# Hashed attention and a convolved feed-forward block on one core: inverse sums by full transposes, key and query loads by head, and a weight's GpSimd part one unit later

## The chip, the cores and the metric

The kernel runs on one NeuronCore of a Trainium2 chip. The metric is the device time of one execution in microseconds (us): the median over three runs is 740.17 us, the runs lying between 739.85 and 744.33.

## What is computed

Attention over 4 batches, 8 heads, 768 positions and head width 64, where a query sees only the keys that fall in its hash bucket (six sign bits of a projection), then a feed-forward block with a three-tap convolution along the sequence. Everything is float32, cut here to what matters:

```python
q_bucket = sum((q @ proj > 0) * 2**arange(6));  k_bucket likewise
scores = where(q_bucket[..., :, None] == k_bucket[..., None, :], q @ k.T / 8, -1e9)
e = exp(scores - max(scores));  x = (e / (sum(e) + 1e-9)) @ v      # (B, S, 512) after joining heads
h = relu(x @ w_in)                                                 # 512 -> 1024
gate = sigmoid(conv_w[0]*h[s-1] + conv_w[1]*h[s] + conv_w[2]*h[s+1])
out = (h * gate) @ w_out                                           # 1024 -> 512
```

The weights arrive as float64 and are decoded on the chip into a high and a low float32 part.

## The kernel before

**Pairs, units and bursts.** Two heads make a pair; there are 16 pairs. A pair has 12 units, k = 0 to 11. A unit is 128 queries of one head against all 768 keys. The main loop (L453) issues, for unit i: the score products of unit i on TensorE (`products`, L257), the row maximum on VectorE, which also moves the scores from PSUM to SBUF (`maximum`, L270), the transposes of unit i-3 on TensorE (L297) with their copy by ScalarE (L304), and the exponential of unit i on ScalarE (L277). Every fourth unit (k = 3, 7 and 11) is a burst: TensorE also multiplies the transposed weights of 256 queries with the values (`values`, L307, 24 matmul records at L325).

**Inverse sums.** For the first seven pairs the division by the sum of exponentials is done after the product with the values. VectorE reduces the partial sums to four numbers per partition and takes their reciprocals (`reciprocals`, L291 and L292, a tile of 128x4), two units ahead of the burst. At the head of the burst, `spread` (L319) lets TensorE bring each of the four columns, broadcast to 64 columns, into the layout of the output: four matmuls of 64 output partitions, two records each. ScalarE copies the result out (L330), VectorE multiplies (`out`, L333), GpSimd splits into a high and a low part (`parts`, L336 and L337). The other nine pairs ("late") divide ahead of the transposes, on GpSimd (`normalise`, L285), and have no spread.

**Preparing the next pair.** The raw queries and keys of the next pair lie in one tile `R` (128 x 2 heads x 768), which has a single buffer. For each head GpSimd makes the high part (L171) and then the low part in place (L176), and SP's DMA queue moves the pieces to where the products read them (L174, L178). The four steps are issued at k = 1, 3, 5 and 7. TensorE computes the hash of both heads at k = 3 (L186), with VectorE's sign test behind it (L189). At k = 7, behind the last low part, SP gets the values' load of the next pair (L165) and then the load of `R` for the pair after it (L158).

**Weights.** The 16 weight blocks are decoded in the background of the first seven pairs. Each block takes six VectorE instructions (L91 to L101), then a cast on ScalarE (L110), then two GpSimd instructions (L111, L112). `background` is called in the bursts, 5.2 steps each (4.2 at k = 3). In a burst GpSimd's queue therefore gets the two weight instructions first, then the `parts` of the output, then the low part of `R`.

**PSUM.** Scores and transposes share three slots in turn, so that the transposes of one unit take the slot of the unit before, and cannot start until VectorE's maximum of that unit has read it.

The feed-forward block of a batch (`ffn`, L412) runs between two units, first when pair 6 is done (221 us into the span).

Of the kernel before, what the change touches and what calls it, by code (L numbers as in the profile page):

```python
# [17 lines left out]
P = 128  # L18
# [3 lines left out]
QB = 256  # L22
# [12 lines left out]
PREP = 1  # L35
PREP_N = 6
W0 = 7
# [5 lines left out]
def lsh_attention_conv_ffn(ctx, tc, qk, v, hw, w_in, conv_w, w_out, consts, ident_in, out):  # L43
# [8 lines left out]
    def ring(pool, bufs, shape, dtype, tag, name):  # L52

        k = turns[tag] = (turns.get(tag, -1) + 1) % bufs
        return pool.tile(shape, dtype, tag=f"{tag}{k}", name=name, bufs=1)
# [47 lines left out]
    def split_weights():  # L103

        while fetched:
            raw, name = fetched.pop(0)
            d = Decode(raw, WC, name)
            yield from d.vector()
            blk = weights[name] = cp.tile([P, 2, WC], F32R, tag=f"w{name}", name=f"w{name}")
            nc.scalar.copy(blk[:, 0, :], d.upf)  # L110
            nc.gpsimd.tensor_tensor(d.upf, d.upf, blk[:, 0, :].bitcast(F32), ALU.subtract)  # L111
            nc.gpsimd.tensor_tensor(blk[:, 1, :], d.upf, d.lowf, ALU.add)  # L112
            yield

# [9 lines left out]
    blocks += [(w_out[f * P:(f + 1) * P], f"o{f}") for f in range(NFC)]  # L124
    fetched, taps, due = [], [], [0]
    weights_todo = split_weights()
# [17 lines left out]
    class Pair:  # L144
        def __init__(self, b, p):
            self.b, self.p, self.nm = b, p, f"{b}_{p}"
            self.late = b * NP + p >= LATE
            self.inv = None

        def load(self):  # L150
            nm = self.nm
            self.R = ring(wp, 1, [P, 2, S], F32R, "R", f"R{nm}")
            src = qk[self.b, 2 * self.p:2 * self.p + 2].rearrange("h p s -> p h s")
            if self.b == self.p == 0:
                for h in range(2):
                    nc.sync.dma_start(self.R[:, h].bitcast(F32), src[:, h])
            else:
                nc.sync.dma_start(self.R.bitcast(F32), src)  # L158
            self.Q1 = ring(wp, 2, [P, 2, S], F32R, "Q1", f"Q1{nm}")
            self.K1 = ring(wp, 2, [P, 2, S], F32R, "K1", f"K1{nm}")  # L160
            self.Q2, self.K2 = Q2s[self.p % 2], K2s[self.p % 2]
# [5 lines left out]
        def split(self, h):  # L167

            lo, R = self.R[:, h], self.R[:, h].bitcast(F32)
            hi = ring(wp, 1, [P, S], F32R, "hi", f"hi{self.nm}_{h}")  # L170
# [9 lines left out]
        def hash(self):  # L180
            hp = ring(ps, 3, [P, 2, 512], F32, "S", f"hash{self.nm}")
            R = self.R.bitcast(F32)
            for h in range(2):
                for half in range(2):
                    g = 32 * (2 * h + half)
                    nc.tensor.matmul(hp[g:g + 32, 0, :HS], hw_sb[:, :32], R[:, h, half * HS:(half + 1) * HS],  # L186
                                     start=True, stop=True, tile_position=(0, g))
# [22 lines left out]
        def prepare_now(self):  # L210
# [3 lines left out]
            for h in range(2):  # L214
                hps.append(ring(ps, 2, [P, 512], F32, "M", f"hash{nm}_{h}")[:, :HS])
                for g in range(4):
                    c, half = 32 * (1 + g // 2), g % 2
                    nc.tensor.matmul(hps[h][32 * g:32 * g + 32], hw_sb[:, c:c + 32],
                                     self.R[:, h, half * HS:(half + 1) * HS].bitcast(F32),
                                     start=True, stop=True, tile_position=(0, 32 * g))  # L220
            for h in range(2):
                R = self.R[:, h].bitcast(F32)
                Q1, Q2, K1, K2 = (t[:, h] for t in (self.Q1, self.Q2, self.K1, self.K2))
# [21 lines left out]
    class Unit:  # L245
# [41 lines left out]
        def reciprocals(self):  # L287

            pr = self.pair
            pr.inv = ring(wp, 2, [P, 2 * QB // P], F32, "inv", f"inv{self.nm}")  # L290
            nc.vector.tensor_reduce(pr.inv, self.sums, mybir.AxisListType.X, ALU.add)  # L291
            nc.vector.reciprocal(pr.inv, pr.inv)  # L292

# [13 lines left out]
    def values(pr, qb, ats, inv):  # L307
# [7 lines left out]
        def spread():  # L315

            for t in range(QB // P):
                for h in range(2):
                    nc.tensor.matmul(av[h * D:(h + 1) * D, QB + t * P:QB + (t + 1) * P],  # L319
                                     inv[:, 2 * t + h:2 * t + h + 1].to_broadcast([P, D]), ident,  # L320
                                     start=True, stop=True, tile_position=(0, h * D))

# [89 lines left out]
    def ffn(b, xs, fill, last):  # L412
# [4 lines left out]
        for i in range(len(todo) + FLAG):  # L417
# [5 lines left out]
            if i == 0:  # L423
                fill()
            background(1)
            if i >= 3:
                prepare(0)
                prepare(1)
# [6 lines left out]
            if i < len(todo):  # L435
# [5 lines left out]
             for t in range(qb * QB // P, (qb + 1) * QB // P)]  # L441
    pairs[0].load()
    nc.sync.dma_start(ident, ident_in)
# [4 lines left out]
    next(first)  # L448
    pairs[1].load()
    av, outs, lows, early = [], [], [], None  # L450
    n = len(units)
    ffn_after = {min((b + 1) * NP - 1 + DEFER, B * NP - 1): b for b in range(B)}
    for i in range(n + LAG):  # L453
# [55 lines left out]
        prepare(1)  # L509
        if u and k == PREP + PREP_N and pi + 1 < len(pairs):  # L510
            pairs[pi + 1].load_v()
            if pi + 2 < len(pairs):
                pairs[pi + 2].load()
        if i == 3:
# [66 lines left out]
```

## Time and profile before

| | |
|---|---|
| runs | 739.85, 740.17, 744.33 us |
| the profiled execution's own time | 739.48 us |
| its span, first to last instruction | 737.5 us |
| TensorE matmul records | 710.9 us busy, 96% of the span |
| VectorE | 487.3 us, 66% |
| ScalarE | 498.5 us, 68% |
| GpSimd | 331.9 us, 45% |
| mean granted TensorE clock | 0.997 |

Engines: PE is TensorE's matmuls, PEld its weight loads, DVE is VectorE, ACT ScalarE, POOL GpSimd, SPq the DMA queue of the sync engine. A share of busy time is a mean over stages; what an engine holds up is read from the waits and from the timeline of a stretch. A row of the timeline gives the start, the time to the end of its last instruction, the engine, the line, the operation, output and inputs, the number of instructions, and in brackets the idle time ahead with what ended it. TensorE's matmuls overlap, so that the distance from one row's start to the next one's start is what a piece of its work costs.

### The profile page before, as it was taken

Reading aid. Unit: us, or ns where it says so; the run is one execution under the profiler, and the core shown is the slowest. Engines: PE = TensorE matmul, PEld = TensorE weight load, DVE = VectorE, ACT = ScalarE, POOL = GpSimd, SP = SyncE. Lnnn points to the kernel's source line nnn. Section 1 sums busy time; section 2 is a strip of 40 time slices with the busy share of each in tenths; the row PEclk is TensorE's granted clock in tenths of the full one; section 3 lists DMA queues with packets and bytes.
Section 4 is the critical chain, followed back from the end, with each engine's and each line's share of the span. In section 5 each row is a group of like instructions: output and inputs, shape, how many; then the busy total and the mean of one; then the engine's idle time right before and its main releaser. Section 6 shows DMA issues by size and latency. Waiting matters only on the chain.

```text
span 737.5 us, 13543 instructions
## 1 busy us (share of the span) xinstructions
PE 710.9 (96%) x4720; PEld 589.0 (80%) x4720; DVE 487.3 (66%) x1211; ACT 498.5 (68%) x937; POOL 331.9 (45%) x334
## 2 busy tenths in 40 slices
PE   6998999899899999999999999999999999999997
PEld 3787777678778988777877998778778899878996
DVE  7977878788775755666665666466666566555663
ACT  5788578678684554877877554778778655585554
POOL 4265456357463522475673532355755232241321
PEclk9999999999999999999999999999999999999999
DMA  4867666663552310237545130324463001100011
GB/s 143 222 187 202 165 186 166 165 166 89 147 146 52 86 44 36 72 77 189 139 105 149 34 94 3 108 60 113 117 180 95 1 0 44 44 1 1 0 44 43
DMA packets 30355, 72.17 MB, mean 98 GB/s; under 512 B 5936, under 2 KB 7504, under 8 KB 30288
## 3 DMA queue, kind: packets, MB, share of 16 engines
q1 hardware_dynamic: 27696, 62.88, 32.0%
q10 hardware_dynamic: 2592, 8.44, 3.3%
q8 instruction: 37, 0.61, 0.3%
q14 instruction: 30, 0.25, 0.1%
HBM read 27.40 MB, written 6.29 MB: 46 GB/s over the span
## 4 chain that ended last, share of the span: by engine, by line
PE 69%; DMA 11%; POOL 7%; issue 5%; DVE 4%; SPq 3%; ACT 1%; POOLq 0%; DVEq 0%; ACTq 0%
PE h L368 19%; PE o L398 18%; PE v L325 11%; PE s L257 10%; PE t L297 9%; DMA R<-in_qk 6%; DMA k<-R 4%; POOL R L176 2%; SPq L174 2%; DVE e L270 1%; DMA K<-hi 1%; PE hash L186 1%; POOL hi L171 1%; ACT e L277 1%; SPq L178 1%
## 5 line engine op out<-in xcount | busy, mean ns | idle before, releaser
L270 DVE TENSOR_SCALAR_CACHE_REDUCE e<-s 128x768 f32<-128x768 f32 x192 | 183.2, 954 | 81.2 <-PE s L257 70.6
L277 ACT ACTIVATE e<-e,st 128x768 f32<-128x768 f32 x192 | 181.3, 944 | 10.3 <-DVE st L284 5.0
L304 ACT COPY at<-t 128x768 f32<-128x768 f32 x192 | 152.3, 794 | 47.0 <-PE t L297 47.0
L297 PE MATMUL t<-ident,e 128*128 128x128 f32 x1152 | 160.0, 275 | 3.6 <-POOL e L285 1.5
L377 DVE SCALAR_TENSOR_TENSOR ht<-ht,cw 128x384 f32<-128x384 f32 (+1 forms) x128 | 114.7, 896 | 71.2 <-ACT ht L375 69.0
L387 POOL TENSOR_TENSOR g<-ht,g 128x384 fp32r<-128x384 f32 x64 | 71.5, 1117 | 179.5 <-ACT g L386 141.8
L297 PEld LDWEIGHTS t<-ident,e 128*128 128x128 f32 x1152 | 130.6, 141 | 22.3 <-POOL e L285 7.4
L285 POOL TENSOR_SCALAR e<-e,st 128x768 f32<-128x768 f32 x108 | 98.3, 911 | 103.1 <-DVE st L284 51.4
L398 PE MATMUL o<-wo,g 128*128 128x512 f32 x576 | 142.4, 394 | 0.0
L368 PE MATMUL h<-xh,wi 128*128 128x386 f32 x512 | 141.9, 340 | 0.0
L325 PE MATMUL v<-at,v 128*64 128x256 f32 x1152 | 135.6, 385 | 0.0
L398 PEld LDWEIGHTS o<-wo,g 128*128 128x128 f32 x576 | 107.4, 188 | 20.3
L257 PE MATMUL s<-K,Q 128*128 128x384 f32 x384 | 116.7, 385 | 1.9 <-ACT e L277 1.0
L325 PEld LDWEIGHTS v<-at,v 128*64 128x64 f32 x1152 | 81.2, 138 | 42.4 <-issue 8.6
L257 PE MATMUL s<-k,q 96*128 96x384 f32 x384 | 100.2, 342 | 2.1 <-ACT q L237 1.9
L368 PEld LDWEIGHTS h<-xh,wi 128*128 128x128 f32 x512 | 94.1, 188 | 4.8 <-issue 1.8
L380 ACT ACTIVATE ht<-ht 128x384 f32<-128x384 f32 x64 | 33.6, 526 | 91.4 <-DVE ht L377 91.4
L368 PE MATMUL h<-xl,wi 128*128 128x386 f32 x256 | 86.7, 339 | 0.0
L257 PEld LDWEIGHTS s<-K,Q 128*128 128x128 f32 x384 | 59.0, 192 | 23.2 <-issue 16.6
L257 PEld LDWEIGHTS s<-k,q 96*128 96x128 f32 x384 | 70.7, 191 | 3.5 <-ACT q L237 3.0
L381 DVE TENSOR_TENSOR ht<-ht 128x384 f32<-128x384 f32 x64 | 40.2, 629 | 33.4 <-ACT ht L380 33.4
L176 POOL TENSOR_TENSOR R<-R,hi 128x768 fp32r<-128x768 f32 x30 | 56.6, 1886 | 0.2
(75 smaller groups left out, 586.0 us busy)
## 6 DMA issues: line engine op xcount, KB each, us to landing
R<-in_qk SPq DMA_DIRECT2D x15, 768.0 KB
K<-hi SPq DMA_DIRECT2D x60, 192.0 KB
v<-in_v SPq DMA_DIRECT2D x16, 384.0 KB
out<-osb SPq DMA_DIRECT2D x24, 256.0 KB
Q<-hi SPq DMA_DIRECT2D x30, 192.0 KB
q<-hi SPq DMA_DIRECT2D x30, 192.0 KB
Q<-R SPq DMA_DIRECT2D x30, 192.0 KB
k<-R SPq DMA_DIRECT2D x30, 192.0 KB
```

The lines of the kernel that those rows point to most:

```text
L176: nc.gpsimd.tensor_tensor(lo, R, hi.bitcast(F32), ALU.subtract)
L257: nc.tensor.matmul(self.sp[:, half, :HS], A[:, h, qs], C[:, h, half * HS:(half + 1) * HS], start=(kk == 0), stop=(kk == 1))
L270: nc.vector.tensor_scalar(self.e.rearrange("p (a b) -> p a b", a=2), self.sp[:, :, :HS], MASKED, None, ALU.max, ALU.max, accum_out=self.st ...
L277: nc.scalar.activation(self.e, self.e, AF.Exp, bias=self.st[:, 1:2], scale=SCALE, accum_out=self.sum)
L285: nc.gpsimd.tensor_scalar(self.e, self.e, self.st[:, 3:4], 0.0, ALU.mult, ALU.add)
L297: nc.tensor.transpose(self.tp[:, c // 3, c % 3 * P:(c % 3 + 1) * P], self.e[:, c * P:(c + 1) * P], ident)
L304: nc.scalar.copy(pr.at[self.h][:, :, :, self.tq * P:(self.tq + 1) * P], self.tp[:, :, :3 * P].rearrange("p j (c q) -> p j c q", c=3))
L325: nc.tensor.matmul(av[h * D:(h + 1) * D, :QB], vt[:, c, h, :], ats[h][:, c // 3, c % 3, :], start=(c == 0), stop=(c == NCK - 1), tile_posi ...
L368: nc.tensor.matmul(hp[:, :HW], w, x[:, c0:c0 + HW], start=(n == 0), stop=(n == 3 * NCC - 1))
L377: nc.vector.scalar_tensor_tensor(t[:, a:z], ht[:, o + k - 1 + a:o + k - 1 + z], cw[:, f, k:k + 1], t[:, a:z], ALU.mult, ALU.add)
L387: nc.gpsimd.tensor_tensor(g[:, 1, :], t, g[:, 0, :].bitcast(F32), ALU.subtract)
L398: nc.tensor.matmul(op, l, r, start=(f == 0 and n == 0), stop=(f == NFC - 1 and n == 2))
```

## The change

There are three parts.

1. `reciprocals` now writes the four reciprocals spread out: the sums go to a tile `total` of 128x4, and one VectorE reciprocal reads it with each number broadcast 64 times and writes a tile `inv` of 128x256. `spread` is two transposes of 128x128 instead of four matmuls of 64 output partitions.
2. `R` is two tiles, one per head. Their loads are issued at k = 7 and k = 8, and the values' load moves behind the second. The hash reads the two tiles in turn.
3. A weight block's two GpSimd instructions are taken out of the burst: the cast puts the block on a list `cast`, and `low_weights` issues them at the end of the next unit that isn't a burst (in the feed-forward block at once).

```diff
-PREP_N = 6
+PREP_N = 6,7
...
             nc.scalar.copy(blk[:, 0, :], d.upf)
+            cast.append((d, blk))
+            yield
+
+    def low_weights():
+
+        for d, blk in cast:
             nc.gpsimd.tensor_tensor(d.upf, d.upf, blk[:, 0, :].bitcast(F32), ALU.subtract)
             nc.gpsimd.tensor_tensor(blk[:, 1, :], d.upf, d.lowf, ALU.add)
-            yield
+        cast.clear()
...
-        def load(self):
+        def load(self, h):
+
             nm = self.nm
-            self.R = ring(wp, 1, [P, 2, S], F32R, "R", f"R{nm}")
-            src = qk[self.b, 2 * self.p:2 * self.p + 2].rearrange("h p s -> p h s")
-            if self.b == self.p == 0:
-                for h in range(2):
-                    nc.sync.dma_start(self.R[:, h].bitcast(F32), src[:, h])
-            else:
-                nc.sync.dma_start(self.R.bitcast(F32), src)
+            self.R[h] = ring(wp, 1, [P, S], F32R, f"R{h}", f"R{nm}_{h}")
+            nc.sync.dma_start(self.R[h].bitcast(F32), qk[self.b, 2 * self.p + h])
+            if h == 0:
+                return
...
         def reciprocals(self):
 
             pr = self.pair
-            pr.inv = ring(wp, 2, [P, 2 * QB // P], F32, "inv", f"inv{self.nm}")
-            nc.vector.tensor_reduce(pr.inv, self.sums, mybir.AxisListType.X, ALU.add)
-            nc.vector.reciprocal(pr.inv, pr.inv)
+            total = ring(wp, 2, [P, 2 * QB // P], F32, "total", f"total{self.nm}")
+            nc.vector.tensor_reduce(total, self.sums, mybir.AxisListType.X, ALU.add)
+
+            pr.inv = ring(wp, 1, [P, QB], F32, "inv", f"inv{self.nm}")
+            nc.vector.reciprocal(pr.inv.rearrange("p (a d) -> p a d", d=D),
+                                 total.unsqueeze(2).to_broadcast([P, 2 * QB // P, D]))
...
             for t in range(QB // P):
-                for h in range(2):
-                    nc.tensor.matmul(av[h * D:(h + 1) * D, QB + t * P:QB + (t + 1) * P],
-                                     inv[:, 2 * t + h:2 * t + h + 1].to_broadcast([P, D]), ident,
-                                     start=True, stop=True, tile_position=(0, h * D))
+                nc.tensor.transpose(av[:, QB + t * P:QB + (t + 1) * P], inv[:, t * P:(t + 1) * P], ident)
...
         prepare(1)
-        if u and k == PREP + PREP_N and pi + 1 < len(pairs):
+        if not burst:
+            low_weights()
+        if u and k - PREP in PREP_N and pi + 2 < len(pairs):
+            pairs[pi + 2].load(PREP_N.index(k - PREP))
+        if u and k - PREP == PREP_N[1] and pi + 1 < len(pairs):
             pairs[pi + 1].load_v()
-            if pi + 2 < len(pairs):
-                pairs[pi + 2].load()
```

How the instructions stand on three queues follows. A name carries the number of its pair within the batch, or of its weight block, and ends in a serial number.

GpSimd's queue from a burst at k = 3 to the burst at k = 7, where the next pair, the first of batch 1, is being prepared. Before:

```order
L111 TENSOR_TENSOR upi_1_1199<-upi_1_1199,wi_1_1320 128x512
L112 TENSOR_TENSOR wi_1_1320<-upi_1_1199,lowi_1_1198 128x512
L336 TENSOR_SCALAR xh_2_1030<-rs_2_1_1154 128x256
L337 TENSOR_TENSOR xl_2_1031<-rs_2_1_1154,xh_2_1030 128x256
L176 TENSOR_TENSOR R_0_1089<-R_0_1089,hi_0_0_1247 128x768
L191 TENSOR_SCALAR bits_0_1299<-bits_0_1299,cst 128x384
L171 TENSOR_SCALAR hi_0_1_1383<-R_0_1089 128x768
L111 TENSOR_TENSOR upi_1_1325<-upi_1_1325,wi_1_1453 128x512
L112 TENSOR_TENSOR wi_1_1453<-upi_1_1325,lowi_1_1324 128x512
L336 TENSOR_SCALAR xh_2_1030<-rs_2_2_1272 128x256
L337 TENSOR_TENSOR xl_2_1031<-rs_2_2_1272,xh_2_1030 128x256
L176 TENSOR_TENSOR R_0_1089<-R_0_1089,hi_0_1_1383 128x768
```

After:

```order
L341 TENSOR_SCALAR xh_2_1032<-rs_2_1_1157 128x256
L342 TENSOR_TENSOR xl_2_1033<-rs_2_1_1157,xh_2_1032 128x256
L181 TENSOR_TENSOR R_0_0_1085<-R_0_0_1085,hi_0_0_1249 128x768
L196 TENSOR_SCALAR bits_0_1301<-bits_0_1301,cst 128x384
L117 TENSOR_TENSOR upi_1_1198<-upi_1_1198,wi_1_1320 128x512
L118 TENSOR_TENSOR wi_1_1320<-upi_1_1198,lowi_1_1197 128x512
L176 TENSOR_SCALAR hi_0_1_1384<-R_0_1_1110 128x768
L341 TENSOR_SCALAR xh_2_1032<-rs_2_2_1274 128x256
L342 TENSOR_TENSOR xl_2_1033<-rs_2_2_1274,xh_2_1032 128x256
L181 TENSOR_TENSOR R_0_1_1110<-R_0_1_1110,hi_0_1_1384 128x768
L117 TENSOR_TENSOR upi_1_1323<-upi_1_1323,wi_1_1452 128x512
L118 TENSOR_TENSOR wi_1_1452<-upi_1_1323,lowi_1_1322 128x512
```

The two parts of the output and the low part of `R` now stand ahead of the weight's two instructions, and no longer behind the cast that these wait for.

SP's DMA queue at k = 7 and 8 of the same pair: the last two pieces of the pair that is being prepared, then the loads. Before:

```order
L178 DMA Q_3_719<-R_3_717 64x768
L178 DMA k_1_82<-R_3_717 64x768
L165 DMA v_3_1087<-in_v 128x768
L158 DMA R_0_1089<-in_qk 128x2x768
L174 DMA Q_0_1091<-hi_0_0_1247 64x768
```

After:

```order
L183 DMA Q_3_741<-R_3_1_739 64x768
L183 DMA k_1_82<-R_3_1_739 64x768
L161 DMA R_0_0_1085<-in_qk 128x768
L161 DMA R_0_1_1110<-in_qk 128x768
L170 DMA v_3_1114<-in_v 128x768
L179 DMA Q_0_1112<-hi_0_0_1249 64x768
```

The load of `R` is two loads of half the size, both ahead of the values' load, and the first needs nothing of the two pieces ahead of it (it overwrites the other head's tile).

VectorE's queue around `reciprocals` of pair 1, between the maxima of three units. Before:

```order
L270 TENSOR_SCALAR e_1_5_0_748,st_1_5_0_747<-s_1_5_0_742 128x768
L274 TENSOR_SCALAR st_1_5_0_747<-st_1_5_0_747 128x1
L291 TENSOR_REDUCE inv_1_3_1_751<-sums_74 128x4
L292 RECIPROCAL inv_1_3_1_751<-inv_1_3_1_751 128x4
L270 TENSOR_SCALAR e_1_4_1_769,st_1_4_1_768<-s_1_4_1_763 128x768
```

After:

```order
L275 TENSOR_SCALAR e_1_5_0_751,st_1_5_0_750<-s_1_5_0_745 128x768
L279 TENSOR_SCALAR st_1_5_0_750<-st_1_5_0_750 128x1
L296 TENSOR_REDUCE total_1_3_1_754<-sums_74 128x4
L299 RECIPROCAL inv_1_3_1_756<-total_1_3_1_754 128x256
L275 TENSOR_SCALAR e_1_4_1_773,st_1_4_1_772<-s_1_4_1_767 128x768
```

They keep their places; the reciprocal writes 256 elements per partition where it wrote four.

More of the change, by code (lines that the diff above doesn't have):

```diff
@@ L124, in lsh_attention_conv_ffn @@
     blocks += [(w_out[f * P:(f + 1) * P], f"o{f}") for f in range(NFC)]
-    fetched, taps, due = [], [], [0]
+    fetched, cast, taps, due = [], [], [], [0]
     weights_todo = split_weights()
@@ L146, in __init__ @@
             self.b, self.p, self.nm = b, p, f"{b}_{p}"
+            self.R = [None, None]
             self.late = b * NP + p >= LATE
             self.inv = None
-        def load(self):
+        def load(self, h):
             nm = self.nm
-            self.R = ring(wp, 1, [P, 2, S], F32R, "R", f"R{nm}")
-            src = qk[self.b, 2 * self.p:2 * self.p + 2].rearrange("h p s -> p h s")
-            if self.b == self.p == 0:
-                for h in range(2):
-                    nc.sync.dma_start(self.R[:, h].bitcast(F32), src[:, h])
-            else:
-                nc.sync.dma_start(self.R.bitcast(F32), src)
+            self.R[h] = ring(wp, 1, [P, S], F32R, f"R{h}", f"R{nm}_{h}")
+            nc.sync.dma_start(self.R[h].bitcast(F32), qk[self.b, 2 * self.p + h])
+            if h == 0:
+                return
             self.Q1 = ring(wp, 2, [P, 2, S], F32R, "Q1", f"Q1{nm}")
@@ L167, in split @@
         def split(self, h):
-            lo, R = self.R[:, h], self.R[:, h].bitcast(F32)
+            lo, R = self.R[h], self.R[h].bitcast(F32)
             hi = ring(wp, 1, [P, S], F32R, "hi", f"hi{self.nm}_{h}")
@@ L181, in hash @@
             hp = ring(ps, 3, [P, 2, 512], F32, "S", f"hash{self.nm}")
-            R = self.R.bitcast(F32)
             for h in range(2):
+                R = self.R[h].bitcast(F32)
                 for half in range(2):
                     g = 32 * (2 * h + half)
-                    nc.tensor.matmul(hp[g:g + 32, 0, :HS], hw_sb[:, :32], R[:, h, half * HS:(half + 1) * HS],
+                    nc.tensor.matmul(hp[g:g + 32, 0, :HS], hw_sb[:, :32], R[:, half * HS:(half + 1) * HS],
                                      start=True, stop=True, tile_position=(0, g))
@@ L218, in prepare_now @@
                     nc.tensor.matmul(hps[h][32 * g:32 * g + 32], hw_sb[:, c:c + 32],
-                                     self.R[:, h, half * HS:(half + 1) * HS].bitcast(F32),
+                                     self.R[h][:, half * HS:(half + 1) * HS].bitcast(F32),
                                      start=True, stop=True, tile_position=(0, 32 * g))
             for h in range(2):
-                R = self.R[:, h].bitcast(F32)
+                R = self.R[h].bitcast(F32)
                 Q1, Q2, K1, K2 = (t[:, h] for t in (self.Q1, self.Q2, self.K1, self.K2))
@@ L441, in lsh_attention_conv_ffn @@
              for t in range(qb * QB // P, (qb + 1) * QB // P)]
-    pairs[0].load()
+    for h in range(2):
+        pairs[0].load(h)
     nc.sync.dma_start(ident, ident_in)
@@ L448, in lsh_attention_conv_ffn @@
     next(first)
-    pairs[1].load()
+    for h in range(2):
+        pairs[1].load(h)
     av, outs, lows, early = [], [], [], None
@@ L509, in lsh_attention_conv_ffn @@
         prepare(1)
-        if u and k == PREP + PREP_N and pi + 1 < len(pairs):
+        if not burst:
+            low_weights()
+        if u and k - PREP in PREP_N and pi + 2 < len(pairs):
+            pairs[pi + 2].load(PREP_N.index(k - PREP))
+        if u and k - PREP == PREP_N[1] and pi + 1 < len(pairs):
             pairs[pi + 1].load_v()
-            if pi + 2 < len(pairs):
-                pairs[pi + 2].load()
         if i == 3:
```

## Prediction, written before the changed kernel ran

> **What bounds the kernel now.** I read the page's first table, then the windows of 20 us, then the waits, then the timeline of single stretches.
>
> ```profile
> PE 710.9 (96%) x4720; PEld 589.0 (80%) x4720; DVE 487.3 (66%) x1211; ACT 498.5 (68%) x937; POOL 331.9 (45%) x334
> ```
> ```profile
> 100.00:120.00 20.00, 19.51 (x161) 15.70 (x160) 16.69 (x47) 15.79 (x32) 10.70 (x11) 1.00 0.50 145
> 120.00:140.00 20.00, 17.16 (x140) 13.09 (x138) 15.72 (x33) 12.76 (x25) 11.42 (x13) 1.00 0.81 225
> 400.00:420.00 20.00, 20.00 (x111) 18.23 (x107) 12.71 (x17) 10.24 (x21) 7.11 (x6) 1.00 0.16 38
> ```
>
> TensorE (the second figure) fills its windows behind 221 us, and nothing that the change touches waits there, so nearly all of the effect must fall in the first seven pairs. There VectorE (fourth figure) is busy for 16 to 17 of 20 us: little room for more work on it. The waits name what holds TensorE and GpSimd in this stage:
>
> ```profile
> POOL upi L111 <- ACT wi L110: 35.9, 8, 8.7
> POOL upo L111 <- ACT wo L110: 27.6, 8, 6.0
> PE hash L186 <- DMA R<-in_qk: 9.1, 9, 2.2
> ```
>
> GpSimd stands for 63.5 us behind casts that aren't done, and TensorE for 9.1 us behind the load of queries and keys. The two hang together, as the timeline around the burst that begins at 112.75 (k = 7) shows. First TensorE:
>
> ```profile
> 110.57 0.84 PE L297 MATMUL t<-ident,e 128*128 128x128 f32 x6
> 111.19 0.62 PE L257 MATMUL s<-K,Q 128*128 128x384 f32 x2
> 112.00 0.82 PE L297 MATMUL t<-ident,e 128*128 128x128 f32 x6
> 112.75 0.66 PE L319 MATMUL v<-ident,inv 128*64 128x128 f32 x8
> 113.24 2.76 PE L325 MATMUL v<-at,v 128*64 128x256 f32 x24
> 115.93 0.62 PE L257 MATMUL s<-K,Q 128*128 128x384 f32 x2
> ```
>
> Next VectorE, from the reciprocal ahead of that burst to the first maximum behind it:
>
> ```profile
> 110.59 0.15 DVE L291 TENSOR_REDUCE inv<-sums 128x4 f32<-128x8 f32 x1
> 110.78 0.18 DVE L292 RECIPROCAL inv<-inv 128x4 f32<-128x4 f32 x1
> 110.87 0.93 DVE L270 TENSOR_SCALAR_CACHE_REDUCE e<-s 128x768 f32<-128x768 f32 x1
> 112.20 0.96 DVE L270 TENSOR_SCALAR_CACHE_REDUCE e<-s 128x768 f32<-128x768 f32 x1 [0.21 <-PE s L257]
> 113.27 0.41 DVE L333 TENSOR_TENSOR rs<-v,rs 128x256 f32<-128x256 f32 x1
> 113.61 0.87 DVE L93 TENSOR_SCALAR lowi<-lowi 128x512 f32<-128x512 f32 x1
> 117.10 0.95 DVE L270 TENSOR_SCALAR_CACHE_REDUCE e<-s 128x768 f32<-128x768 f32 x1
> ```
>
> Two margins matter. The maximum of 110.87 ends at 111.80 and the transposes that need its slot start at 112.00. And the six decode instructions from 113.61 end at 117.10, while the scores of 115.93 were ready at 116.94 (a maximum starts 1.01 behind its scores: 111.19 and 112.20). VectorE has no slack at either place. GpSimd, last:
>
> ```profile
> 113.36 0.83 POOL L171 TENSOR_SCALAR hi<-R 128x768 fp32r<-128x768 f32 x1
> 117.58 1.29 POOL L111 TENSOR_TENSOR upi<-upi,wi 128x512 f32<-128x512 f32 x1 [3.39 <-ACT wi L110]
> 118.95 1.28 POOL L112 TENSOR_TENSOR wi<-upi,lowi 128x512 fp32r<-128x512 f32 x1
> 120.20 0.41 POOL L336 TENSOR_SCALAR xh<-rs 128x256 fp32r<-128x256 f32 x1
> 120.69 0.73 POOL L337 TENSOR_TENSOR xl<-rs,xh 128x256 fp32r<-128x256 f32 x1
> 121.38 1.82 POOL L176 TENSOR_TENSOR R<-R,hi 128x768 fp32r<-128x768 f32 x1
> ```
> ```profile
> 123.76 5.43 DMA k<-R
> 128.85 0.59 PE L257 MATMUL s<-K,Q 128*128 128x384 f32 x2 [1.01 <-ACT e L277]
> 133.70 0.85 PE L186 MATMUL hash<-R,hw_sb 128*32 128x384 f32 x8 [1.82 <-DMA R<-in_qk]
> ```
>
> While VectorE decodes (113.61 to 117.10), GpSimd waits for the cast. The low part of R is done at 123.2, its transfer lands at 129.2, only then does the next load of R start, and the hash comes 1.82 late. The scores at 128.85 are the first of the second head, whose pieces that transfer carries; I take their 1.01 for the same lateness.
>
> **The reciprocal (part 1).** It grows from 4 to 256 elements per partition. No such instruction is in the trace; these groups are nearest:
>
> ```profile
> L292 DVE RECIPROCAL inv<-inv 128x4 f32<-128x4 f32 x21 | 3.7, 178 | 0.7
> L284 DVE RECIPROCAL st<-st 128x1 f32<-128x1 f32 x108 | 17.5, 162 | 0.0
> L281 DVE TENSOR_SCALAR st<-st 128x1 f32<-128x1 f32 x108 | 16.5, 153 | 15.0 <-ACT e L277 14.7
> L333 DVE TENSOR_TENSOR rs<-v,rs 128x256 f32<-128x256 f32 x21 | 8.7, 416 | 2.1 <-ACT rs L330 2.1
> ```
>
> Low end: it runs like the product of 256 elements, 0.42 us. High end: each element costs what the reciprocal of one costs above another operation on one, 162 - 153 = 9 ns, so 0.153 + 256 x 0.009 = 2.46 us. Between them lies the reciprocal's own slope, (178 - 162) / 3 = 5.3 ns: 0.178 + 252 x 0.0053 = 1.51 us. I take 1.45, a little less, since a slope over three elements is rough to some 10%: 1.27 more than now. It stands at a place without slack. The maximum of 110.87 would start at 112.14 and end at 113.07, and the transposes of 112.00 come 1.1 late. VectorE does this 21 times; once or so TensorE waits for something else meanwhile, so 20 x 1.1 = +22 us. At the low end 0.24 more leaves some 0.1 each, +2; at the high end 2.28 more and 2.1 each, +42.
>
> The Trainium skill (VectorE: DVE Perf Modes, First, the fixed hardware budget) says that a reciprocal is an iterative divide with a repeat count of 8. At that page's 0.96 GHz and eight cycles per element, an estimate by it is some 2.3 us for 256 elements, and the sum below would end near 785. The slope of 5.3 ns doesn't bear out eight cycles, though it rules out one.
>
> **The transposes (part 1).** A spread now costs 112.75 to 113.24 plus what the step into it takes: transposes to spread 0.75, spread to values 0.49, so 1.24 in all. In a late pair transposes go straight to values in 0.77:
>
> ```profile
> 307.31 0.85 PE L297 MATMUL t<-ident,e 128*128 128x128 f32 x6
> 308.08 2.81 PE L325 MATMUL v<-at,v 128*64 128x256 f32 x24
> ```
>
> Six transposes take 0.62 from 110.57 to 111.19, so two more take 0.2, together 0.97: TensorE saves 0.27 per spread, 21 x 0.27 = 5.7 us. But what follows the values on TensorE waits for VectorE's decode (no slack at 117.10); where that gets later, the saving is lost. I count 0, and 5.7 if VectorE doesn't decide.
>
> **GpSimd's order (part 3) and the loads (part 2).** The output's parts (0.41 and 0.73) and the low part of R (1.82) no longer wait for the cast, so they now run while VectorE decodes. That isn't free. Where they met so far, each held the other up:
>
> ```profile
> 135.68 2.00 POOL L176 TENSOR_TENSOR R<-R,hi 128x768 fp32r<-128x768 f32 x1
> 136.04 1.93 DVE L93 TENSOR_SCALAR lowo<-lowo 128x512 f32<-128x512 f32 x1
> 140.36 0.88 PE L297 MATMUL t<-ident,e 128*128 128x128 f32 x6 [0.36 <-DVE e L270]
> 30.86 0.87 PE L297 MATMUL t<-ident,e 128*128 128x128 f32 x6 [0.59 <-DVE e L270]
> ```
>
> The decode step of 136.04 ended 0.29 behind GpSimd's low part (137.68) and took 1.93; the one of 113.61 took 0.87 beside the high part of 113.36. They take turns, instruction by instruction. Without the 0.44 lost there, the six steps of 113.61 to 117.10 are 3.05, 0.51 each. So in the changed kernel:
> - At k = 7, 5.2 steps (2.65) and GpSimd's 2.96 in turns end 5.6 behind 113.61, at 119.2: 2.3 later than the scores are ready. With 0.1 of margin the transposes come 2.2 late. Six such bursts, and the first one, without output parts (1.1), which loses 0.6 already (30.86): +13.7.
> - At k = 11, 2.65 + 1.14 = 3.8, at 117.4: 0.4 late, six times, +2.4.
> - At k = 3 the burst is longer by the hash. The row at 140.36 is this very case, with some 0.4 of idle time. Four bursts of six are new to it: +1.6.
>
> Together +17.7. If decode and GpSimd don't hold each other up there, 0. The weight's own two instructions, 2.6 us, move under the maxima of the next unit, whose scores come from PSUM; maxima beside GpSimd's instructions take their usual 0.93 to 0.96 (110.87, 112.20), so I cost them at nothing.
>
> In return R comes early. At k = 7 its low part ends some 5 us sooner (118 and not 123.2), the first head's load waits for nothing but its turn on SP's queue, the second for a landing of 4 to 5.5 us, then half of the 768 KB. All that fits ahead of the hash, 8 units on. That removes the 9.1, the 1.0 of 128.85, and the slow stretch behind the longest of these waits, where a burst's values took 4.45 instead of 2.76:
>
> ```profile
> 74.78 4.45 PE L325 MATMUL v<-at,v 128*64 128x256 f32 x24
> ```
>
> 9.1 + 1.0 + 1.7 = -11.8. The values' load, now last, is first used at k = 7 of the next pair; the 11 units ahead of that cover it.
>
> **The sum.** From the profiled execution's 739.5: +22 +17.7 -11.8 = 767.4, and with the 0.7 that the median of the runs, 740.2, lies above it, 768 us.
>
> **The rivals.**
> - A: the reciprocal runs one element per cycle like other operations. For it: the operation is a single pass in name. Against: 178 and 162 ns. 740.2 + 2 + 17.7 - 11.8 = 748.
> - B: GpSimd's work in the burst doesn't decide, as where its instructions fall between VectorE's. Against it: the rows at 136.04 and 113.61. Then the transposes' saving counts: 740.2 + 22 - 11.8 - 5.7 = 745.
> - C: both, so that TensorE sets the pace and all its waits for R vanish: 740.2 + 2 - 11.8 - 5.7 = 725. This is the faster side; it needs a reciprocal under some 0.5 us and no turns on the decode.
> - D: the reciprocal costs 9 ns per element: 740.2 + 42 + 17.7 - 11.8 = 788.
> - That the loads aren't early, because SP still waits in order ahead of them, would put 11.8 on the forecast: 780. The low part ends 5 us sooner, which speaks against it.
>
> **How the numbers follow.** Forecast 0.55, A 0.15, B 0.12, C 0.10, D 0.05, loads still late 0.03. The terms' own uncertainty (a tenth on the slope, a third on the turns) puts the forecast at 754 to 782. The range, 740 to 783, takes in A and B and leaves out C and D. A difference under 1% can't be told from none here: below 732.8 lies C with a little of B, 0.11; between 732.8 and 747.6 B and half of A, 0.19; above, 0.70.
>
> **What would show it.** Right: the reciprocal's group at about 1450 ns; VectorE's maximum as what the transposes ahead of each burst wait for; decode groups with means well over 0.51 us; hardly any wait of the hash for R and of GpSimd for casts; the span up to the first feed-forward block at about 248 us, not 221, and the rest unchanged. Wrong: a reciprocal under 0.5 us, or decode steps at their present times beside GpSimd's low part; above all a TensorE without idle time in the first seven pairs.

## The result, and the profile after

The changed kernel takes 768.25 us (four runs, 767.84 to 770.45), the kernel before on the same chip 740.78 (four runs, 739.85 to 744.33). The ratio is 1.0368, with a 95% interval of 1.0328 to 1.0408: 27.5 us slower. The forecast was 768. One execution of part 3 alone (e3 below), the only one of it with a trace, took 2459 us with matmuls two to three times as long as elsewhere, and counts nowhere below.

The profiled execution took 768.21 us and spans 766.4. The first row of the first feed-forward block shows where the time was lost. In the kernel before, and then in the changed one:

```profile
220.95 0.44 PE L368 MATMUL h<-xh,wi 128*128 128x386 f32 x1
```
```profile
252.42 0.45 PE L373 MATMUL h<-xh,wi 128*128 128x386 f32 x1
```

The first seven pairs take 31.5 us more; from there to the end of the span it is 514.0 us instead of 516.6: in four of the late pairs TensorE stood idle ahead of the hash before, 2.1 us in all, and doesn't now. The first table and the windows of the changed kernel:

```profile
PE 714.2 (93%) x4594; PEld 585.7 (76%) x4594; DVE 544.1 (71%) x1211; ACT 500.4 (65%) x937; POOL 341.1 (45%) x334
```
```profile
100.00:120.00 20.00, 15.49 (x104) 12.28 (x102) 18.85 (x37) 13.14 (x25) 7.84 (x8) 0.91 0.59 162
120.00:140.00 20.00, 17.07 (x126) 13.32 (x124) 19.52 (x34) 12.51 (x26) 13.28 (x12) 1.00 0.55 158
```

VectorE went from 16 or 17 busy microseconds in 20 to 19 or more, and TensorE is idle for 3 to 4.5. The waits turn over with it:

```profile
POOL xh L341 <- DVE rs L338: 99.9, 21, 12.1
...
PEld t L305 <- DVE e L275: 45.8, 35, 2.4
PE t L305 <- DVE e L275: 35.0, 31, 2.1
...
POOL upo L117 <- ACT wo L110: 7.2, 4, 2.5
POOL upi L117 <- ACT wi L110: 7.0, 5, 2.5
```

GpSimd stands for casts for 14.2 us, where it was 63.5 before, and the hash's wait for `R` is gone from the list. TensorE's transposes now wait for VectorE's maxima. The timeline shows both places where this happens, ahead of a burst (118.11) and at the second transposes behind one (114.14). TensorE, then VectorE, then GpSimd:

```profile
112.19 0.52 PE L262 MATMUL s<-k,q 96*128 96x384 f32 x2
114.14 0.87 PE L305 MATMUL t<-ident,e 128*128 128x128 f32 x6 [1.44 <-DVE e L275]
...
115.56 0.82 PE L305 MATMUL t<-ident,e 128*128 128x128 f32 x6
...
118.11 0.87 PE L305 MATMUL t<-ident,e 128*128 128x128 f32 x6 [1.00 <-DVE e L275]
```
```profile
109.40 0.96 DVE L91 TENSOR_SCALAR lowi<-rawi 128x512 int32<-128x512 int32 x1
110.39 1.40 DVE L93 TENSOR_SCALAR lowi<-lowi 128x512 f32<-128x512 f32 x1
111.83 1.39 DVE L95 TENSOR_SCALAR lowi<-lowi 128x512 int32<-128x512 int32 x1
113.14 0.94 DVE L275 TENSOR_SCALAR_CACHE_REDUCE e<-s 128x768 f32<-128x768 f32 x1
...
115.48 1.75 DVE L299 RECIPROCAL inv<-total 128x256 f32<-128x256 f32 x1
117.15 0.90 DVE L275 TENSOR_SCALAR_CACHE_REDUCE e<-s 128x768 f32<-128x768 f32 x1
```
```profile
109.03 1.05 POOL L342 TENSOR_TENSOR xl<-rs,xh 128x256 fp32r<-128x256 f32 x1
110.21 1.29 POOL L117 TENSOR_TENSOR upi<-upi,wi 128x512 f32<-128x512 f32 x1
111.58 1.34 POOL L118 TENSOR_TENSOR wi<-upi,lowi 128x512 fp32r<-128x512 f32 x1
```

Ahead of the burst the reader sees the reciprocal, 1.75 us of VectorE, and the maximum behind it, which ends at 118.05; the transposes start at 118.11. Behind the burst the decode steps of 110.39 and 111.83 take 1.4 us each, about as long as GpSimd's instructions of 110.21 and 111.58 run; without GpSimd the mean of a step was 0.51. The maximum of 113.14 ends at 114.08, the transposes start at 114.14.

Transposes that wait for nothing start 0.35 behind the second row of their scores. What goes beyond that, summed over all rows up to the first feed-forward block, is their lateness. With the other distances from row to row on TensorE (from 30 us on) the 31.5 us divide so:

| us | before | after | difference |
|---|---|---|---|
| transposes late ahead of a burst | 0.0 | 20.8 | +20.8 |
| transposes late, second behind a burst | 1.9 | 19.5 | +17.6 |
| transposes to hash, 7 times | 13.8 | 5.6 | -8.2 |
| transposes to spread, spread to values, values to scores | 71.8 | 67.4 | -4.4 |
| the rest: the first 30 us, and scores behind late transposes | | | +5.7 |

### The profile page after: what moved, and what is told of

It is laid out like the page before. It is cut to its first block, busy times and chain, and to the rows that moved or that the text cites. A ratio compares the mean times of both kernels' runs of the same rounds, so it can differ in the third digit from the quotient of the medians.

```text
span 766.4 us, 13352 instructions
## 1 busy us (share of the span) xinstructions
PE 714.2 (93%) x4594; PEld 585.7 (76%) x4594; DVE 544.1 (71%) x1211; ACT 500.4 (65%) x937; POOL 341.1 (45%) x334
## 4 chain that ended last, share of the span: by engine, by line
PE 71%; DVE 22%; issue 2%; DMA 2%; POOL 1%; ACT 1%; SPq 0%; ACTq 0%; DVEq 0%; POOLq 0%
PE h L373 18%; PE o L403 17%; PE t L305 12%; PE v L330 11%; PE s L262 11%; DVE e L275 7%; DVE inv L299 3%; PE hash L191 2%; DVE upi L97 1%; DVE lowi L95 1%; DMA Q<-R 1%; DVE lowi L99 1%; DVE lowo L93 1%; DVE lowo L91 1%; DVE st L279 1%
## 5 line engine op out<-in xcount | busy, mean ns | idle before, releaser
L305 PE MATMUL t<-ident,e 128*128 128x128 f32 x1152 | 164.5, 280 | 37.3 <-DVE e L275 35.0
L330 PEld LDWEIGHTS v<-at,v 128*64 128x64 f32 x1152 | 79.5, 137 | 47.7 <-issue 10.9
L181 POOL TENSOR_TENSOR R<-R,hi 128x768 fp32r<-128x768 f32 x30 | 59.5, 1983 | 3.7 <-PE hash L191 3.6
```

Of the source, the lines that this page charges most:

```text
L181: nc.gpsimd.tensor_tensor(lo, R, hi.bitcast(F32), ALU.subtract)
L305: nc.tensor.transpose(self.tp[:, c // 3, c % 3 * P:(c % 3 + 1) * P], self.e[:, c * P:(c + 1) * P], ident)
L330: nc.tensor.matmul(av[h * D:(h + 1) * D, :QB], vt[:, c, h, :], ats[h][:, c // 3, c % 3, :], start=(c == 0), stop=(c == NCK - 1), tile_posi ...
```

## The experiments

Each ratio is to the kernel before on the same chip: 742.5 us for e1 to e3 and e23, 740.9 for e5 to e8, 743.2 for e9 to e12. The times are medians; the ratios are taken over all runs and can differ from theirs in the third decimal.

| experiment | us | ratio and interval |
|---|---|---|
| e1: part 1 alone | 752.68 | 1.0137 (1.0098 to 1.0176) |
| e2: part 2 alone | 734.46 | 0.9881 (0.9820 to 0.9943) |
| e3: part 3 alone | 746.52 | 1.0053 (1.0030 to 1.0075) |
| e23: parts 2 and 3 | 747.89 | 1.0055 (1.0028 to 1.0082) |
| e9: parts 1 and 2 | 752.63 | 1.0128 (1.0097 to 1.0160) |
| e8: the change, copy then wide reciprocal | 781.55 | one run |
| e12: the change, narrow reciprocal and copy | 751.95 | 1.0114 (1.0080 to 1.0148) |
| e10: part 2, narrow reciprocal, VectorE copy, transposes | 738.66 | 0.9942 (0.9922 to 0.9962) |
| e11: part 2, narrow reciprocal, ScalarE copy, transposes | 734.19 | 0.9881 (0.9854 to 0.9909) |
| e5: parts 2 and 3, GpSimd's rest of a burst queued later | 759.97 | 1.0240 (1.0197 to 1.0284) |
| e6: e5 with narrow reciprocal, copy, transposes | 765.68 | 1.0309 (1.0262 to 1.0355) |
| e7: e5 with part 1 | 782.13 | 1.0543 (1.0505 to 1.0580) |

**The parts alone.** The edits are those of the change's diff, one part at a time.

> Part 1 alone: the wide reciprocal and the two transposes, with the loads and GpSimd's order of before. Theory (the wide reciprocal holds up the next maximum, and the transposes ahead of each burst with it): some 1.45 us at 20 bursts, +29, since VectorE isn't behind from the decode here; the hash comes later by that, so that most of the waits for R (up to 11) are hidden; 752 to 763 us, best guess 757. Rival (only the turns between decode and GpSimd cost anything, the reciprocal is hidden behind the matmuls): 735, less than before by the transposes' 5.7.

> Part 2 alone: R in two tiles, loaded ahead of the values, GpSimd's order as before. Theory (R is late because GpSimd's low part is late, and because the load is queued behind the values' and is large): the low part stays late, the half loads land some 1 to 2 us earlier than the whole one did, most of the hash's waits of 1.5 to 2.2 go: 732 to 737. Rival (only GpSimd's lateness counts): no difference, 740.

> Part 3 alone: a weight's two GpSimd instructions one unit later. Theory (the output's parts and R's low part now take turns with VectorE's decode): +17.6 of late transposes two units behind the bursts, -11 of waits for R: 744 to 749. Rival (GpSimd's work out of the cast's way is free, only the reciprocal costs): 729 to 732.

All three came within the ranges expected. Part 2 alone is faster than both kernels. The three ratios add up to +0.7%, 5 us, and together they cost 27.5. The distance from transposes to hash explains most of the gap: 13.8 us before, but 5.6 with part 1 alone and 5.5 with part 2 alone. Part 1 makes every pair longer, and in the longer pair the load of `R` is no longer late. So part 1 alone gets back about 8 us that the loads would get back in any case, and this gain can be had only once. (Part 2 alone still waits for the second tile within the hash, 1.6 us in all.) That part 3 alone gets it too (there `R`'s low part runs earlier) is argued, from the 13.4 us that part 3 adds where part 2 is already there.

**Two parts at a time.** Part 3 without the wide reciprocal, and the wide reciprocal without part 3.

> Parts 2 and 3 without part 1. Theory: as part 3 alone, since R is early enough already there: 744 to 749, some 20 to 25 below the changed kernel; transposes two units behind a burst still late by about 18 in all, those of the burst itself not. Rival (the reciprocal makes all of the loss): 729 to 732.

> Parts 1 and 2 without part 3: wide reciprocal, transposes and loads by head, with GpSimd's weight instructions in the burst behind the cast as before. If part 3 costs what parts 2 and 3 together (747.9) cost over part 2 alone (734.5), some 13 us, this is about 755 (752 to 759): 734.5, plus about 22 for the reciprocal with its two transposes (part 1 alone came to +12 net of 9 to 10 us of waits for the queries and keys, which are gone here already). The transposes two units behind a burst are not late, those ahead of a burst by 1.2 to 1.4 us each. Rival: beside the wide reciprocal part 3 costs little, because VectorE is late anyway: then this is within 5 us of the whole change, 763 to 768.

Both hold. On top of part 2, part 3 costs 747.89 - 734.46 = 13.4 us, and part 1 costs 752.63 - 734.46 = 18.2 (17.5 when each is set against the kernel before on its own chip). Both prices share the uncertainty of part 2's time, some 4.5 us by its interval. They sit at different places. With part 3 (e23) transposes are late by 0.5 us ahead of bursts and 17.4 at the second place behind; with part 1 (e9) by 27.7 and 1.7. And only part 3 makes the decode longer. One step of it in part 2 alone, in parts 1 and 2, in parts 2 and 3, and in the whole change:

```profile
L99 DVE TENSOR_SCALAR lowi<-upi 128x512 int32<-128x512 int32 x8 | 3.4, 424 | 0.2
```
```profile
L99 DVE TENSOR_SCALAR lowi<-upi 128x512 int32<-128x512 int32 x8 | 3.4, 425 | 0.2
```
```profile
L99 DVE TENSOR_SCALAR lowi<-upi 128x512 int32<-128x512 int32 x8 | 6.3, 782 | 0.2
```
```profile
L99 DVE TENSOR_SCALAR lowi<-upi 128x512 int32<-128x512 int32 x8 | 7.7, 959 | 0.2
```

The step itself is the same in all four: 424 and 425 ns, then 782 and 959. A single step can be beside GpSimd in one kernel and not in another, so the sum over all 96 decode steps of the weight blocks is the better measure: 58.9 us and 56.9, then 87.1 and 87.3 (59.5 in the kernel before). The wide reciprocal adds nothing to it, GpSimd's earlier work adds 28 us. That shuts out rival B. Together the three prices, -8.1, +13.4 and +18.2, are 23.5 of the 27.5 us; the other 4, no more than the uncertainty of part 2's time, are not attributed.

**What makes the reciprocal slow.** The change both widens the reciprocal and lets it read each number 64 times. Here a copy broadcasts first, and the reciprocal then reads and writes 256 plain elements.

```diff
-            nc.vector.reciprocal(pr.inv.rearrange("p (a d) -> p a d", d=D),
-                                 total.unsqueeze(2).to_broadcast([P, 2 * QB // P, D]))
+            nc.vector.tensor_copy(pr.inv.rearrange("p (a d) -> p a d", d=D),
+                                  total.unsqueeze(2).to_broadcast([P, 2 * QB // P, D]))
+            nc.vector.reciprocal(pr.inv, pr.inv)
```

> The changed kernel with the broadcast done by a VectorE copy first, and the reciprocal of 256 elements in place, read without a broadcast. Theory (each element of a reciprocal costs six cycles or so): the reciprocal still takes 1.75 us, the copy comes on top: 770 to 778 us. Rival (reading one number 64 times is what is slow): the reciprocal falls below 0.9 us and the time below 760.

The groups, of the changed kernel and of this one:

```profile
L299 DVE RECIPROCAL inv<-total 128x256 f32<-128x256 f32 x21 | 36.8, 1753 | 0.7
```
```profile
L299 DVE COPY inv<-total 128x256 f32<-128x256 f32 x21 | 10.0, 476 | 0.7
...
L301 DVE RECIPROCAL inv<-inv 128x256 f32<-128x256 f32 x21 | 36.8, 1753 | 0.7
```

The reciprocal's time is the same to the nanosecond, so it is the number of elements and not the way they are read. The kernel came out 3.6 us above the expected range: the transposes ahead of bursts are late by 33.7 us, 12.9 more than in the change, against 10.0 us of copies.

**The same change without a wide reciprocal.** The division is done on 4 elements, and a VectorE copy broadcasts the result.

```diff
+            nc.vector.reciprocal(total, total)
-            nc.vector.reciprocal(pr.inv.rearrange("p (a d) -> p a d", d=D),
-                                 total.unsqueeze(2).to_broadcast([P, 2 * QB // P, D]))
+            nc.vector.tensor_copy(pr.inv.rearrange("p (a d) -> p a d", d=D),
+                                  total.unsqueeze(2).to_broadcast([P, 2 * QB // P, D]))
```

> The whole change with one thing other: a reciprocal of 4 elements and a VectorE copy that broadcasts it (0.48 us), in place of the wide reciprocal (1.75 us). Theory (the wide reciprocal costs 1.0 us in each of 20 bursts, and GpSimd's turns with the decode the rest): the transposes ahead of the bursts are 0.3 late, those two units behind them still some 16 us in all; 748 to 753, where the lower end holds if the transposes' saving of 5.7 us counts. Rival: the reciprocal isn't what makes the change slow, and the time stays at 763 to 768.

As expected: 16.3 us come back (768.25 - 751.95). The transposes ahead of bursts are late by 5.1 us instead of 20.8, those behind by 18.5 instead of 19.5. So the width of the reciprocal is by far the larger part of what part 1 costs.

**Can the transposes pay?** They need the inverses spread out, at VectorE's cost. First the narrow reciprocal with a VectorE copy on top of part 2 (the diff above); then the copy on ScalarE in the burst, with the transposes behind the values.

> Part 2, with the reciprocal of 4 elements, a VectorE copy that broadcasts them to 256 (0.48 us), and the two transposes. Against part 2 alone (734.5): the copy makes the transposes ahead of each burst 0.2 to 0.3 us late, 20 times, +4 to +6; the transposes save 0.27 in 21 spreads, -5.7, if the saving reaches the end. Theory: 733 to 736. Rival: the saving is lost because VectorE's decode sets when the first maximum behind a burst starts: 738 to 741.

> Part 2, with the reciprocal of 4 elements on VectorE, the broadcast copy on ScalarE at the start of the burst (ahead of the cast, where ScalarE idles for 1.6 us), and the two transposes at the end of the burst's values. VectorE gets no work more than before. If the transposes' saving of 5.7 us reaches the end: 729 (727 to 731). If it is lost because VectorE's decode sets the first maximum behind the burst, which in part 2 alone starts as the last decode step ends: 734.5 (733 to 736). Over 737: ScalarE's copy delays the cast or the next copy out of PSUM.

```diff
+        def widen():
+            nc.scalar.copy(wide.rearrange("p (a d) -> p a d", d=D),
+                           inv.unsqueeze(2).to_broadcast([P, 2 * QB // P, D]))
...
-        return [spread, *chunks], (factors, out, parts)
+        return [lambda: (widen(), chunk(0)), *chunks[1:], spread], (factors, out, parts)
```

With VectorE's copy the time is 4.2 us over part 2 alone (the intervals touch), in the rival's range, but not for the rival's reason. The copy takes 581 ns here, and transposes ahead of bursts are late by 8.8 us, where 4 to 6 were expected. The saving is smaller than expected and is not lost. A burst of the changed kernel, from its transposes to the next scores:

```profile
94.13 0.87 PE L305 MATMUL t<-ident,e 128*128 128x128 f32 x6 [1.00 <-DVE e L275]
94.84 0.38 PE L326 MATMUL v<-ident,inv 128*128 128x128 f32 x2
95.15 2.81 PE L330 MATMUL v<-at,v 128*64 128x256 f32 x24
97.89 0.62 PE L262 MATMUL s<-K,Q 128*128 128x384 f32 x2
```

That is 0.71, 0.31 and 2.74, together 3.76, where the burst of 112.00 before took 0.75, 0.49 and 2.69, together 3.93. A spread by transposes saves 0.17 us there; in the bursts that begin with the hash it is 3.89 for 3.96, a saving of 0.07. Over the 19 bursts behind 30 us that is 2.7 us, and e10 shows the same 3.76. With the transposes behind the values (e11) most bursts take some 3.85, and those with the hash 3.71 where it doesn't wait, some 3 us less in all. Yet e11 ties with part 2 alone. The hash's waits for `R`, in part 2 alone and then in e11, tell where the saving goes:

```profile
PEld hash L185 <- DMA R<-in_qk: 1.6, 3, 0.8
```
```profile
PEld hash L185 <- DMA R<-in_qk: 3.4, 4, 1.2
PE hash L185 <- DMA R<-in_qk: 1.8, 4, 0.9
```

5.2 us against 1.6: the load is late again by about as much as the bursts save. (The changed kernel has no such wait.) So it isn't VectorE's decode that takes the saving, as far as these two traces show. No kernel here was faster than these two.

**Moving GpSimd's work further.** If GpSimd's work beside the decode costs 13 us, moving the output's parts and the low part of `R` to the unit behind the burst should save it.

```diff
-PREP_N = 6,7
+PREP_N = 6,8
...
-            return steps((None, None, hs, hs)), steps((sa, None, sa, None, sb, None, sb))
+            return steps((None, None, hs, hs)), steps((sa, None, None, sa, sb, None, None, sb))
...
-        for last in parts:
-            last()
+        held += parts
+        if not burst:
+            for last in held:
+                last()
+            held = []
```

> Parts 2 and 3, reciprocal and spread as before, and GpSimd's other work of a burst (the output's parts, the low part of R) also moved to the unit behind it, where VectorE reads scores from PSUM; the second half of R is loaded at k = 9. Theory (decode and GpSimd take turns): the late transposes two units behind a burst shrink from 15.7 to 2 to 4, the hash doesn't wait for R: 728 to 733 us. Rival (the loss of 5.4 without the reciprocal comes from the order of the loads, or of the weights): no gain against parts 2 and 3, 744 to 749.

> As the run before, with the two transposes, but the reciprocal of four numbers, and a VectorE copy that broadcasts them to 256. Theory (a wide reciprocal is dear by its elements, a copy isn't): the copy takes 0.3 to 0.45 us, of which up to 0.2 a burst is late, against 0.27 saved by the transposes: 724 to 731 us. Rival (any VectorE instruction of 256 elements at this place costs as much as the reciprocal): 745 to 755.

> The changed kernel with GpSimd's work moved behind the burst, the wide reciprocal kept. Theory (two separate losses): 768 less some 16 of turns, 748 to 755 us, about what part 1 alone gave, with 1.0 to 1.4 of late transposes at each of the 20 bursts. Rival (the two losses share their time, VectorE being full either way): 758 or more.

All three missed, by 27 to 35 us, for two reasons that I had not thought of. The first shows in GpSimd's rows of e5, beside one decode step of VectorE, and in the low part of `R` at the same burst of e23:

```profile
117.85 0.51 POOL L341 TENSOR_SCALAR xh<-rs 128x256 fp32r<-128x256 f32 x1 [0.98 <-DVE rs L338]
118.44 0.79 POOL L342 TENSOR_TENSOR xl<-rs,xh 128x256 fp32r<-128x256 f32 x1
119.19 2.27 POOL L181 TENSOR_TENSOR R<-R,hi 128x768 fp32r<-128x768 f32 x1
```
```profile
119.81 1.93 DVE L99 TENSOR_SCALAR lowi<-upi 128x512 int32<-128x512 int32 x1
```
```profile
122.30 2.27 POOL L181 TENSOR_TENSOR R<-R,hi 128x768 fp32r<-128x768 f32 x1
```

These instructions are queued one unit later, but nothing stands ahead of them in GpSimd's queue, so they start when their input is there: in the same burst, beside the same decode. The low part starts 1.88 us behind the burst's values in e5 (117.31) and 1.87 in e23 (120.43). At the burst of k = 7 the second transposes are late by 10.2 us in both; only at k = 3 did the move help (1.4 instead of 5.4), and in all they are late by 13.8 us. A later place in a queue is a later time only if something ahead of it takes time or waits. In the kernel before, that something was the wait for the cast. The second reason is the larger part of the miss, 17.3 us: the late pairs got slower. From the first feed-forward row to the end e5 takes 531.5 us and not 514.2 as in e23 (e6 531.4, e7 532.5), while up to that row it takes 226.7 us, 5.5 less than e23. In the late pairs the low part of `R`, issued at k = 4 and 8, runs on the engine that also divides (`normalise`), and the transposes wait for the division. In e23 these two waits are 7.4 and 1.5 us; in e5:

```profile
PEld t L302 <- POOL e L290: 24.5, 26, 1.9
PE t L302 <- POOL e L290: 17.7, 16, 1.6
```

On this basis the reciprocals stand to each other as elsewhere: the wide one adds 22.2 us (e7 against e5), the narrow one with its copy 5.7 (e6).

## Why the prediction was right, and where it was wrong

**Which stage pays.** Forecast: the first feed-forward block at 248 us instead of 221, the rest unchanged. Measured: 252.4, and the rest 2.6 us shorter. That nothing the change touches waits there was not quite true: 2.1 us ahead of the hash did. That the total came out within 0.3 us of 768 is luck; the terms below were off by more, and what no term named was +5.7.

**The reciprocal, +22.** Measured: +20.8. The mechanism and the place are right, and one rate was wrong: 1.45 us per instruction by the slope from 1 to 4 elements, where it takes 1.75. By that price alone the lateness should be 1.4 per burst, 28 us in 20, and where part 3 is absent it is (1.40 to 1.45 in most bursts of e1 and e9, 27.3 and 27.7 us in all). In the whole change it is 1.1 or 1.2 in nine of 20 bursts, 1.3 to 1.5 in seven, 0.8 in one and nothing in three. What decides shows when one sets the reciprocal against the transposes beside it, in e1 and then (rows of 115.48 and 115.56 above) in the change:

```profile
106.79 1.75 DVE L294 RECIPROCAL inv<-total 128x256 f32<-128x256 f32 x1
```
```profile
106.67 0.82 PE L300 MATMUL t<-ident,e 128*128 128x128 f32 x6
```

In e1 the reciprocal starts 0.12 behind these transposes and the next ones come 1.37 late, in the change it starts 0.08 ahead of them and they come 1.17 late. So it is throughout: with a start 0.07 or 0.08 ahead the lateness is 1.12 to 1.17 in e1, e9 and the change alike, with one 0.17 to 0.24 behind it is 1.40 to 1.51, but for three bursts. That VectorE starts earlier in the change because TensorE had just waited for it, so that its scores lay ready, is argued and not shown. The three bursts that aren't late at all (106.66, 174.94 and 243.55) are those right behind a stretch of half clock (last section), and there the reciprocal starts 0.9 to 1.2 us ahead of the transposes. So two errors cancelled by luck, a price 0.3 too low and a lateness taken as independent of the turns. Rival A (under 0.5 us) and D (2.46) are shut out by 1753 ns.

**The turns, +17.7.** Measured: +17.6, and 13.4 as a price in e23 against e2. That sum is better than its parts, which is luck again. At the second transposes behind the burst of k = 7, where I said 2.2 in each of six, they are late by 1.1 to 2.2, 10.3 in all (13.2 forecast); at k = 3 by 0.4 to 1.6, 5.6 in all (1.6 forecast); at k = 11 by 1.6 or 1.7 in two bursts and by 0.1 or less in the others (3.4 in all, 2.4 forecast). One step failed outright: the weight's two instructions, costed at nothing because they would fall under maxima. The rows of 110.21 and 111.58 fall beside decode steps that VectorE had not done yet, and hold these to 1.4 us each. Where a schedule is late, what was moved out of the crowded stretch finds it still crowded.

The Trainium skill (SBUF — State Buffer, Who interferes with whom) says that VectorE and GpSimd share one pair of ports, that in VectorE's two-port modes whoever issues first holds it for a whole instruction, and that the other is blocked. The rows here agree, though none shows a step's mode: 1.93 us for a step of 0.42 (e5 at 119.81) beside a GpSimd instruction that itself grows from 1.82 to 2.27.

**The loads, -11.8.** Measured on their own: -8.1 (e2). The hash's part is -8.2 in the change up to the first feed-forward block, and -2.1 in the late pairs. The stretch of slow values at 74.78 went away as forecast, but three of its kind came, which I did not foresee (last section).

**The transposes, 0.** In size this was wrong in two ways that cancel: a spread saves 0.17 and not 0.27, since the values start 0.31 behind it and not 0.2, and follow more slowly by 0.05; behind the hash it saves 0.07; and this is not lost, as e10's rows show. Of the table's -4.4, 1.7 are the slow stretch of 74.78 and the other 2.7 these transposes.

**The rest.** No term named the +5.7. Some 2 of them, by estimate from the distances between rows, are scores behind late transposes, most of them at half clock (last section). 2.3 are one wait within the values of the first burst; in the change and in part 2 alone:

```profile
29.08 2.80 PE L330 MATMUL v<-at,v 128*64 128x256 f32 x22 [2.30 <-ACT at L312]
```
```profile
28.70 2.80 PE L324 MATMUL v<-at,v 128*64 128x256 f32 x22 [3.15 <-ACT at L303]
```

The kernel before and part 1 alone don't have it, so the loads bring it, as part 2 places them (e5 to e7, which load the second head two units behind the first, don't have it either). What TensorE waits for is a copy of ScalarE, and the profile puts that copy's delay down to the landing of a piece of the queries:

```profile
28.22 0.80 ACT L312 COPY at<-t 128x768 f32<-128x768 f32 x1 [4.33 <-DMA Q<-R]
```

Why that piece lands later was not followed, and the other 1.4 us of the rest are not attributed. Since the hash's wait for `R` is gone, the rival of late loads is out, and with a slow reciprocal and real turns C is out too.

## What to carry to other kernels

Before an operation is widened to save TensorE a few tenths, look for its cost per element: a reciprocal is slow in proportion to its elements, so divide the few and copy the result to the many, on an engine with room (e11), and even that only breaks even here. A wait on an engine off the critical path can be what keeps it away from another engine's port; taking it out moves its work, and the place where that work lands must be priced too. When parts of a change are timed one by one, ask whether two of them are credited with the same wait.

## What the runs showed of the hardware

- A VectorE reciprocal costs 1753 ns for 256 elements per partition and 178 for 4: (1753 - 178) / 252 = 6.25 ns per element, with plain and with broadcast input. The Trainium skill (VectorE: DVE Perf Modes, First, the fixed hardware budget) gives a reciprocal a repeat count of 8. At that page's clock of 0.96 GHz and one cycle per repeat this would be 8.3 ns, an estimate; the measurement comes to six such cycles.
- TensorE's clock halves behind some idle times. In the changed kernel it happened three times behind the first 20 us, behind the idle times of 2.07, 1.77 and 2.04 us. Before, it happened once, behind the hash's wait of 2.18 us at 73.51, which is the slow stretch of 74.78; the waits of 1.82 and 1.87 had no such effect. The first of the three, in windows of 2 us (the clock is the third figure from the end) and on TensorE:

```profile
100.00:102.00 2.00, 0.21 (x2) 0.00 (x0) 2.00 (x2) 0.36 (x1) 1.92 (x2) 1.00 1.06 272
102.00:104.00 2.00, 1.72 (x9) 1.72 (x10) 1.90 (x8) 1.49 (x3) 0.47 (x1) 0.69 1.02 264
104.00:106.00 2.00, 2.00 (x10) 1.90 (x9) 2.00 (x2) 1.17 (x3) 0.00 (x0) 0.50 0.46 109
106.00:108.00 2.00, 2.00 (x16) 1.73 (x17) 1.45 (x7) 1.99 (x4) 0.00 (x0) 0.96 0.79 309
```
```profile
102.28 1.13 PE L305 MATMUL t<-ident,e 128*128 128x128 f32 x6 [2.07 <-DVE e L275]
104.49 1.48 PE L305 MATMUL t<-ident,e 128*128 128x128 f32 x6
```

  Six transposes take 1.48 us instead of 0.82, and the half clock lasts 3.41 us. In the kernel before it cost 1.7 us of TensorE's time; in the changed one the next reciprocal behind each of the three stretches made nothing late.

  The length of the wait alone doesn't decide, its place does. The three stretches of half clock begin at 102.76, 171.03 and 239.29 us, 20 times 3.413 us apart, and in every other run with several of them they also lie whole multiples of 3.413 us apart. Cut the traces of the nine kernels that show such a stretch behind the first 20 us (the two of this section, e5, e7 to e10, e12 and e23) into steps of 3.413 us that fit their starts, and add up TensorE's idle time in each step. The clock fell to half 19 times, always behind a step with 1.77 us of idle time or more, and never behind one with 1.75 or less. That is why the 2.30 us that end at 29.08 cost no clock (they fall into two steps), and why of two idle times of 2.04 us in e23 one halved it and the other didn't. The Trainium skill (TensorE: Matmul & The Clock Gate, What's actually happening) has the half clock follow an idle window of some 3.4 us; the half rate and the length agree, while here a window that was idle for 1.77 us, about half of it, sufficed.
